# Token-MLP stretches of 25 and 23 filler matmuls, one paired row maximum, and output bursts in two halves

## The chip, the cores and the metric

The kernel runs on 1 core of a Trainium2 chip. The metric is the device time of one execution in microseconds (us). The kernel before was timed three times: 1595.57, 1595.95 and 1596.51, a median of 1595.95. One more execution was profiled and took 1596.58; its span, first instruction to last, is 1594.8.

## The reference, cut to what matters

```python
# S, D, H, F = 2048, 640, 32, 1728; Dh = 20
q = heads(x @ wq); k = x @ wk; v = x @ wv              # one k and one v for all 32 heads
scores = einsum("bhqd,bkd->bhqk", q, k) * Dh ** -0.5
a = rows(einsum("bhqk,bkd->bhqd", softmax(scores), v)) @ wo
h = layernorm(x)
u = gelu(einsum("bsd,sf->bdf", h, w1) + b1)             # MLP over the token axis
b = einsum("bdf,fs->bds", u, w2) + b2
out = g * a + (1 - g) * b                               # g = sigmoid(x . gate_w)
```

## The kernel before, in words

Attention and MLP are woven into one stream. Attention is cut into 512 units (32 blocks of 4 heads x 512 queries, 16 key blocks each), and the stream into 248 *stretches*. A stretch j holds matmuls of four kinds:

- **scores** (L689): keys against queries into one of seven PSUM banks, a tile of 128x512; ScalarE turns it into `p` by an exponential (L701). There are 8 in a stretch.
- **maxima** (L507): the same product with queries in front, so that VectorE can reduce 512 columns to one (`tensor_reduce`, L515). They serve a later block's softmax.
- **fillers**: MLP or output-projection matmuls of 320 columns (L1020 for MLP1, L845 for MLP2, L973 for the projection) into a bank `g` of their own.
- **the burst** (L725): `p` times V for two units, four heads side by side, into a bank that ScalarE then copies out (L749) and GpSimd adds up (L752).

Scores, maxima and fillers contract over 64 rows or fewer, so they use one half of the array's rows, and two run side by side. In stretch j the half j % 2 is the *own lane*: it takes the scores and most of the maxima. The other is the *filler lane*: all fillers and one to three maxima. A burst uses all rows, so both lanes end before it.

`ph` lists the fillers of each stretch. `batches` cuts each MLP1 tile (48 steps per lane) into two batches of 24, and each batch gives one stretch per lane: the 70 stretches j = 2 to 71 have 24 fillers each and want 10 maxima (`wants`). MLP2 stretches have 20 or 21 fillers, the projection's 15. `share` says how many maxima the own lane takes (8 of the 10 in MLP1), and `layout` writes each lane's order as a string: `s` score, `m` maximum, `f` filler, `SS` two scores in neighbouring banks with one exponential over 1024 columns. For MLP1 the string is fixed: `ssmSSmmssmssmmmm`.

`arrange` merges the two lanes into TensorE's one queue. It keeps a clock per lane, for VectorE and for ScalarE, and a time at which each bank is free (`free`), all from constants such as `EACH` (an engine's time for one instruction, and how long after its start the bank is free). It issues the lane whose next matmul could start first, in the bank that is free first. A reduction is put on VectorE's queue when its clock says so, or when its bank is taken again. After the last filler, `signal` puts a small memset (L711) on VectorE's queue, for which the next stretch's first filler waits. `burst` takes column ranges (`cuts`): MLP2 bursts are cut into two halves of 256 queries, each with a bank and a copy of its own; MLP1 bursts are whole.

Of the kernel before, what the change touches and what calls it, by code (L numbers as in the profile page):

```python
# [39 lines left out]
def mix_kernel(ctx: ExitStack, tc: tile.TileContext, A_x, A_wq, A_wk, A_wv, A_wo,  # L40
# [452 lines left out]
    def ms_next(b):  # L493
        k = given[b]
        if k >= 32 * NU or k // 32 not in qtiles:
            return None
        given[b] += 1
        n, r = divmod(k, 32)
        (kq, pr), qt = divmod(r // 4, 2), r % 4

        def step(i=None):
# [10 lines left out]
            out = mtiles[n][:, (2 * b + pr) * 4 + qt, kq:kq + 1]  # L512

            def reduce():
                red = nc.vector.tensor_reduce(out, ms, axis=AX.X, op=ALU.max)  # L515
                if region:
                    touch(red, reads=region)
                issued[b] += 1

            return reduce  # L520

        return step

    def ms_done():
# [504 lines left out]
    def batches(tiles, counts):  # L1029
        out = []  # L1030
        for n, (load, parts, *_) in enumerate(tiles):
            for d, (steps, done) in enumerate(parts):
                cnt = counts.pop(0)
                rows = [[f[h] for f in steps if len(f) > h] for h in range(2)]
                cut = [[len(r) * j // cnt for j in range(cnt + 1)] for r in rows]
                for j in range(cnt):
                    rest = []
                    if d == 0 and j == 0 and n + 1 < len(tiles):
                        rest.append(tiles[n + 1][0])
                    out.append(([r[c[j]:c[j + 1]] for r, c in zip(rows, cut)], rest, [done] if j == cnt - 1 else []))  # L1040
        return out

    n_st = (len(units) - TAIL) // 2
    todo = [divmod(i, FC) for i in range(PRO, 2 * FC)]
    seq = batches([b1_jobs(*t) for t in todo], [2] * len(todo))
    m = len(seq)
    seq += batches([b2_jobs(st) for st in range(NS)], [2] * 2 * NS)
    seq[-1][1].append(second)
# [28 lines left out]
        ph[j][1].append(lambda st=st: tail_load(st, 0, CUT))  # L1077
    ph[n_st - 8][1].append(move_wo)

    X_US, F_US, O_US = 0.2345, 0.1468, 0.869  # L1080
    W_US, FIRST_US, LAST_US, NEXT_US, SEEN_US = 0.11, 0.1, 0.333, 0.13, 0.43
    EACH = {"dve": (0.6, 0.84), "act": (0.48, 0.815)}
    PAIR_US = 0.85
    clock = {"dve": 0.0, "act": 0.0}
    lane, fresh, free = [0.0, 0.0], [True, True], [0.0] * 3 + [1.3] * 4
    state = {"at": 0.0, "f": 0.0, "last": 0.0}
# [13 lines left out]

    def begins(h, kind):
        at = max(lane[h] + W_US * fresh[h], state["at"])
        if kind == "S":
            return max(at, pair[1] if pair else free[next_pair()])
        return max(at, state["f"] if kind in "fe" else min(free))

    def issue(h, kind, f):
        at = state["at"] = begins(h, kind)
        fresh[h] = False
        lane[h] = at + (F_US if kind in "fae" else X_US)  # L1110
        state["last"] = at
        if kind in "fae":
            f()
        elif kind == "S":
            if not pair:
                i = next_pair()
                pair[:] = [i, free[i + 1]]
                free[i] = free[i + 1] = float("inf")
            else:
                i = pair[0] + 1  # L1120
                begin = spend("act", PAIR_US, at + SEEN_US) - PAIR_US
                free[i - 1] = free[i] = begin + PAIR_US + EACH["act"][1] - EACH["act"][0]
                pair.clear()
            while any(k == i for _, k, _ in reduces):
                reduces.pop(0)[2]()
            f(i)
# [12 lines left out]

    def layout(n_s, n_m, n_f, n_o):  # L1140
        if n_f > 22 and n_o > 1:
            places = [0, n_f]
        elif n_f > 22:
            places = [0]
        else:
            places = [0, n_f]
        places = (places + [n_f // 2, 3 * n_f // 4])[:n_o]
        lf = ""
        for i in range(n_f + 1):
            lf += "m" * places.count(i) + "f" * (i < n_f)  # L1150
        lf += "m" * (n_o - lf.count("m"))
        if n_f > 22 and (n_s, n_m, n_o) == (8, 8, 2):
            return "ssmSSmmssmssmmmm", lf
        lx = "sSS" if n_s + n_m > 12 else "s"
        s, m = n_s - len(lx), n_m
        a, b = s, m
        while s or m:
            if m and (not s or m * a >= s * b):
                lx, m = lx + "m", m - 1
            else:  # L1160
                lx, s = lx + "s", s - 1
        return lx, lf

    def arrange(h, ss, own, other, fs, end):
        ss, own, other, fs = list(ss), list(own), list(other), list(fs)
        n_s, n_m, n_f = len(ss), len(own), len(fs)
        lx, lf = layout(n_s, n_m, n_f, len(other))
        pairs.clear()
        at = lx.replace("m", "").find("S")
        if at >= 0:  # L1170
            pairs.update({at: 0, at + 1: 2})
        lx = [(k, (own if k == "m" else ss).pop(0)) for k in lx]
# [22 lines left out]
    def burst(us, cuts=(0, NB)):  # L1195
# [7 lines left out]
        for at, to in zip(cuts, cuts[1:]):  # L1203
# [9 lines left out]
            free[i] = spend("act", took, t + 0.25) + hold - each  # L1213
        lane[:] = [t + NEXT_US] * 2
        fresh[:] = [True, True]

# [25 lines left out]
    def share(j):  # L1242
        h, to = j % 2, owed + wants[j]
        own = round((min(to, 9) + F_US / X_US * len(ph[j][0]) - 8) / 2)
        if h:
            own = (given[0] - given[1] + to + 1) // 2
        own = min(to, max(0, own))
        return (to - own, own) if h else (own, to - own)

    for j in range(n_st):  # L1250
# [31 lines left out]
        w1_load(fetched[0] + 3)  # L1282
        for f in rest:
            f()
        spend("dve", 0.03)
        spend("act", 0.1)
# [192 lines left out]
```

## Time and profile before

| | us |
|---|---|
| median of three | 1595.95 |
| profiled execution | 1596.58 |
| its span | 1594.8 |
| 70 MLP1 stretches, 187.50 to 611.49 | 423.99 |
| MLP2 stretches, 617.06 to 1316.15 | 699.09 |
| VectorE busy in the MLP1 part | 422.70 |
| ScalarE busy in the MLP1 part | 333.18 |

TensorE counts as busy all the time, because the ends of matmuls are modelled and include their waits; so a stretch is read from starts: of its burst, of the first matmul behind it, of each lane's matmuls, and of the next burst. VectorE's and ScalarE's instructions overlap their successors a little, so what one costs in a full queue is the distance between starts, not its duration.

### The profile page before, as it was taken

Reading aid. Unit: us, or ns where it says so; the run is one execution under the profiler, and the core shown is the slowest. Engines: PE = TensorE matmul, PEld = TensorE weight load, DVE = VectorE, ACT = ScalarE, POOL = GpSimd, SP = SyncE. Lnnn points to the kernel's source line nnn. Section 1 sums busy time; section 2 is a strip of 40 time slices with the busy share of each in tenths; the row PEclk is TensorE's granted clock in tenths of the full one; section 3 lists DMA queues with packets and bytes.
Section 4 is the critical chain, followed back from the end, with each engine's and each line's share of the span. In section 5 each row is a group of like instructions: output and inputs, shape, how many; then the busy total and the mean of one; then the engine's idle time right before and its main releaser. Section 6 shows DMA issues by size and latency. Waiting matters only on the chain.

```text
span 1594.8 us, 43452 instructions
## 1 busy us (share of the span) xinstructions
PE 1587.7 (100%) x16907; PEld 1184.8 (74%) x16907; DVE 1381.2 (87%) x2626; ACT 1295.5 (81%) x2481; POOL 846.0 (53%) x930
## 2 busy tenths in 40 slices
PE   9999999999999999999999999999999999999998
PEld 7799867767676777777777777777777776666665
DVE  6689999999999999999999999999999996677743
ACT  4445678778787788888888888888888889999996
POOL 6558767777777777545544344444444433333340
PEclk9999999999999999999999999999999999999999
DMA  7665322232222221322112122122211113322341
GB/s 213 204 173 144 97 60 71 66 75 69 77 64 70 61 76 54 93 70 66 52 55 58 53 61 58 55 61 62 62 54 49 48 49 101 118 84 83 90 138 59
DMA packets 180452, 129.78 MB, mean 81 GB/s; under 512 B 41617, under 2 KB 150062, under 8 KB 180246
## 3 DMA queue, kind: packets, MB, share of 16 engines
q1 hardware_dynamic: 179958, 126.68, 28.4%
q8 instruction: 133, 2.18, 0.6%
q14 instruction: 73, 0.60, 0.1%
q10 hardware_dynamic: 288, 0.33, 0.1%
HBM read 93.57 MB, written 32.15 MB: 79 GB/s over the span
## 4 chain that ended last, share of the span: by engine, by line
PE 97%; DVE 1%; SPq 1%; DMA 1%; POOL 0%; ACT 0%; issue 0%; DVEq 0%
PE xs L725 30%; PE xs L689 18%; PE xs L507 18%; PE g L845 11%; PE g L1020 7%; PE pu L634 4%; PE pp L303 3%; PE g L973 3%; PE x L507 1%; PE xs L927 1%; DMA xa<-in_A_x_dram 0%; DVE st L236 0%; SPq L200 0%; DMA q_scr<-ql 0%; PE pt L295 0%; DVE ht L255 0%
## 5 line engine op out<-in xcount | busy, mean ns | idle before, releaser
L515 DVE TENSOR_REDUCE mp<-xs 128x1 f32<-128x512 f32 x1946 | 1199.8, 683 | 130.2 <-PE xs L689 66.6
L701 ACT ACTIVATE p<-xs 128x512 f32<-128x512 f32 (+1 forms) x1841 | 1016.1, 674 | 7.3 <-PE xs L689 3.4
L752 POOL TENSOR_TENSOR osum<-osum,part 128x512 f32<-128x512 f32 x216 | 279.7, 1295 | 594.2 <-ACT part L749 577.6
L725 PE MATMUL xs<-p,v_sb 128*32 128x256 f32 (+1 forms) x6144 | 493.6, 454 | 0.0
L689 PE MATMUL xs<-q,kst 62*128 62x512 f32 x1344 | 474.0, 416 | 0.0
L507 PE MATMUL xs<-kst,q 60*128 60x512 f32 x1242 | 432.9, 408 | 0.0
L725 PEld LDWEIGHTS xs<-p,v_sb 128*32 128x32 f32 x6144 | 173.6, 109 | 209.2 <-issue 80.9
L689 PEld LDWEIGHTS xs<-q,kst 62*128 62x128 f32 x1344 | 237.3, 185 | 57.1 <-DVE mp L515 30.2
L749 ACT ACTIVATE part<-xs 128x256 f32<-128x256 f32 (+1 forms) x328 | 149.1, 455 | 155.6 <-PE xs L725 154.2
L1020 PE MATMUL g<-slot,w 64*128 64x320 f32 x1728 | 266.1, 305 | 0.0
L1020 PEld LDWEIGHTS g<-slot,w 64*128 64x128 f32 x1728 | 258.9, 184 | 1.9
L507 PEld LDWEIGHTS xs<-kst,q 60*128 60x128 f32 x1242 | 214.0, 184 | 50.3 <-DVE mp L515 19.3
L127 POOL TENSOR_TENSOR w<-wr,w 128x512 fp32r<-128x512 f32 (+1 forms) x180 | 225.5, 1255 | 34.6 <-ACT w L124 17.5
L689 PE MATMUL xs<-slot,kst 62*128 62x512 f32 x569 | 207.5, 418 | 0.0
L507 PE MATMUL xs<-kst,slot 60*128 60x512 f32 x576 | 205.5, 408 | 0.0
L845 PE MATMUL g<-u,w 64*128 64x320 f32 x1296 | 200.4, 305 | 0.0
L845 PE MATMUL g<-slot,w 64*128 64x320 f32 x1296 | 200.3, 305 | 0.0
L845 PEld LDWEIGHTS g<-slot,w 64*128 64x128 f32 x1296 | 195.1, 184 | 1.7
L845 PEld LDWEIGHTS g<-u,w 64*128 64x128 f32 x1296 | 195.2, 184 | 1.6
L689 PEld LDWEIGHTS xs<-slot,kst 62*128 62x128 f32 x569 | 100.2, 185 | 19.9 <-ACT part L749 7.4
L507 PEld LDWEIGHTS xs<-kst,slot 60*128 60x128 f32 x576 | 99.7, 184 | 20.3 <-ACT part L749 9.9
L973 PE MATMUL g<-slot 64*128 64x320 f32 x720 | 113.5, 306 | 0.0
(190 smaller groups left out, 1446.4 us busy)
## 6 DMA issues: line engine op xcount, KB each, us to landing
wr<-in_B_w_dram SPq DMA_DIRECT2D x155, 256.0 KB
q<-q_scr SPq DMA_DIRECT2D x126, 80.0 KB
rb<-r_scr SPq DMA_DIRECT2D x120, 64.0 KB
slot<-o_scr SPq DMA_DIRECT2D x24, 320.0 KB
y_scr<-yo SPq DMA_DIRECT2D x16, 320.0 KB
q_scr<-qh SPq DMA_DIRECT2D x19, 256.0 KB
q_scr<-ql SPq DMA_DIRECT2D x19, 256.0 KB
o_scr<-rb SPq DMA_DIRECT2D x120, 40.0 KB
```

The costliest lines, as they stand in the source:

```text
L127: nc.gpsimd.tensor_sub(wl, wr, f32(wh))
L507: mm = nc.tensor.matmul(ms, qtiles[n][64 * b:64 * b + 60, pr, qt * P:(qt + 1) * P], kst[64 * b:64 * b + 60, kq * NB:(kq + 1) * NB], start= ...
L515: red = nc.vector.tensor_reduce(out, ms, axis=AX.X, op=ALU.max)
L634: nc.tensor.matmul(pu[r][:, :HD2], w[rows, c, :], h[rows, st, :], start=(st == 0 and k == 0), stop=(st == NS - 1 and k == 2))
L689: mm = nc.tensor.matmul(s, kst[64 * b:64 * b + 62, kb * P:(kb + 1) * P], q[64 * b:64 * b + 62, pr, :], start=True, stop=True)
L701: act = nc.scalar.activation(p_all[:, a * NB:(j + 1) * NB], s, AF.Exp, scale=SCALE)
L725: mm = nc.tensor.matmul(o[32 * hh:32 * hh + 32, at:to], v_sb[:, units[u][1], :], p_all[:, j * NB + at:j * NB + to], start=first, stop=last ...
L749: touch(nc.scalar.activation(t[:, at:to], o[:, at:to], AF.Copy), [("x", i)])
L752: nc.gpsimd.tensor_add(osum[n], osum[n], t)
L845: other_tile(half, nc.tensor.matmul(hold["p"][:, :HD2], w[r, fc % HS, :], u[d][r, fc, :], start=(hold["n"] == 1), stop=(hold["n"] == 6 * F ...
L973: other_tile(half, nc.tensor.matmul(hold["p"][:, :HD2], o[r, c, :], w[r, c, d * HD2:(d + 1) * HD2], start=(hold["n"] == 1), stop=(hold["n" ...
L1020: other_tile(half, nc.tensor.matmul(hold["p"][:, :HD2], w[r, st % HS, :], h[d][r, st, :], start=(hold["n"] == 1), stop=(hold["n"] == 6 * NS)))
```

## The change

It has these parts.

- `batches` cuts MLP1 tiles into 25 + 23 steps, so that stretches go 25, 25, 23, 23.
- `share` gives the own lane 9 of the 10 maxima beside 25 fillers, and 8 beside 23.
- `layout` has four fixed strings (`EARLY`), by number of fillers and lane. In each, `M` stands for two maxima in neighbouring banks with one `tensor_reduce` over 1024 columns and two outputs. No `SS` is left in MLP1. Where the pair would join two different query blocks' rows (`turns`), `M` changes places with an `m`.
- `burst` is cut into halves in MLP1 too.
- The planner's constants change: banks read by ScalarE are free 0.70 after its start (0.815 before), and others by some hundredths.

```diff
-                cut = [[len(r) * j // cnt for j in range(cnt + 1)] for r in rows]
+                cut = [[len(r) * j // cnt + more * (0 < j < cnt) for j in range(cnt + 1)] for r in rows]
...
+            both = part == 2
+            out = mtiles[n][:, col - both:col + 1, kq]
+            if both:
+                ms = span(i - 1, 2).rearrange("p (a k) -> p a k", a=2)
+                region.append(("x", i - 1))
...
-    X_US, F_US, O_US = 0.2345, 0.1468, 0.869
-    W_US, FIRST_US, LAST_US, NEXT_US, SEEN_US = 0.11, 0.1, 0.333, 0.13, 0.43
-    EACH = {"dve": (0.6, 0.84), "act": (0.48, 0.815)}
-    PAIR_US = 0.85
+    X_US, F_US, O_US = 0.2345, 0.1468, 0.862
+    W_US, FIRST_US, LAST_US, NEXT_US, SEEN_US = 0.11, 0.09, 0.333, 0.112, 0.43
+    EACH = {"dve": (0.598, 0.838), "act": (0.476, 0.70)}
+    PAIR_US = {"act": 0.903, "dve": 1.13}
...
+    EARLY = {(23, 0): "ssmsmssmmsmssMm", (23, 1): "ssmsmsmmsmsssMm",
+             (25, 0): "smsssmssmmmmssmM", (25, 1): "smsssmsmssmMmsmm"}
...
-        if n_f > 22 and (n_s, n_m, n_o) == (8, 8, 2):
-            return "ssmSSmmssmssmmmm", lf
+        if n_f > 22 and (n_s, n_m, n_o) == (8, 10 - n_o, n_o):
+            lx = list(EARLY[n_f, h])
+            at = lx.index("M")
+            if own[lx[:at].count("m")].turns:
+                to = at + 1 if "m" in lx[at:] else max(i for i in range(at) if lx[i] == "m")
+                lx[at], lx[to] = lx[to], lx[at]
+            return "".join(lx).replace("M", "MM"), lf
...
+        if len(ph[j][0]) > 22 and to == 10:
+            own = 8 + (len(ph[j][0]) > 24)
...
-            burst((2 * j - 2, 2 * j - 1), (0, NB // 2, NB) if 15 < len(ph[j][0]) <= 22 else (0, NB))
+            burst((2 * j - 2, 2 * j - 1), (0, NB // 2, NB) if len(ph[j][0]) > 15 else (0, NB))
```

TensorE's queue at the end of one MLP1 stretch, before. In all of these, L507 is a maximum, L689 (now L697) a score, L1020 (L1028) a filler, L725 (L733) the burst; `xs_2756` and `xs_2760` are banks 0 to 2 and 3 to 6.

```order
L507 MATMUL xs_2760<-kst,q 128x512
L1020 MATMUL g<-slot_80,w_90 128x320 x2
L507 MATMUL xs_2756<-kst,slot_79 128x512
L1020 MATMUL g<-slot_80,w_90 128x320
L507 MATMUL xs_2756<-kst,slot_79 128x512
L1020 MATMUL g<-slot_80,w_90 128x320 x2
L507 MATMUL xs_2760<-kst,slot_79 128x512
L507 MATMUL xs_2760<-kst,q 128x512
L725 MATMUL xs_2756<-p,v_sb 32x512 x8
```

The same place of the same stretch now, which is one of 25 fillers.

```order
L697 MATMUL xs_2756<-q,kst 128x512
L1028 MATMUL g<-slot_80,w_90 128x320
L507 MATMUL xs_2756<-kst,slot_79 128x512
L1028 MATMUL g<-slot_80,w_90 128x320 x2
L507 MATMUL xs_2760<-kst,slot_79 128x512
L1028 MATMUL g<-slot_80,w_90 128x320
L507 MATMUL xs_2760<-kst,slot_79 128x512
L1028 MATMUL g<-slot_80,w_92 128x320
L733 MATMUL xs_2760<-p,v_sb 32x256 x16
```

The filler lane now ends with a filler, and the last two maxima of the own lane (both in `xs_2760`) are the pair. The burst has 16 matmuls of 256 columns.

VectorE's queue over one MLP1 stretch, before, from memset to memset (L515 is the reduction).

```order
L711 MEMSET flag 1x1
L515 TENSOR_REDUCE mp<-xs_2760 128x1
L515 TENSOR_REDUCE mp<-xs_2756 128x1 x2
L515 TENSOR_REDUCE mp<-xs_2760 128x1 x2
L515 TENSOR_REDUCE mp<-xs_2756 128x1
L515 TENSOR_REDUCE mp<-xs_2760 128x1 x2
L515 TENSOR_REDUCE mp<-xs_2756 128x1
L515 TENSOR_REDUCE mp<-xs_2760 128x1
L711 MEMSET flag 1x1
```

And now (the reduction is L522, the memset L719).

```order
L719 MEMSET flag 1x1
L522 TENSOR_REDUCE mp<-xs_2760 128x2
L522 TENSOR_REDUCE mp<-xs_2760 128x1
L522 TENSOR_REDUCE mp<-xs_2756 128x1 x2
L522 TENSOR_REDUCE mp<-xs_2760 128x1
L522 TENSOR_REDUCE mp<-xs_2756 128x1
L522 TENSOR_REDUCE mp<-xs_2760 128x1
L522 TENSOR_REDUCE mp<-xs_2756 128x1
L522 TENSOR_REDUCE mp<-xs_2760 128x1
L719 MEMSET flag 1x1
```

Ten reductions became nine; the row `128x2` is the pair. In the MLP2 and projection stretches the four kinds of matmul follow each other as before, in partly other banks. In the last eight visits, which a random search over the planner's clock orders, the order differs.

## Rows read from the trace of the kernel before

**Rows 1.** The page: busy time by engine over the whole span.
```profile
PE 1587.7 (100%) x16907; PEld 1184.8 (74%) x16907; DVE 1381.2 (87%) x2626; ACT 1295.5 (81%) x2481; POOL 846.0 (53%) x930
```

**Rows 2.** Busy time by stretch of time: MLP1, then MLP2.
```profile
core 0: us, PE busy (x) PEld busy (x) DVE busy (x) ACT busy (x) POOL busy (x), PEclk, DMA share, GB/s
187.50:611.49 423.99, 423.99 (x4062) 300.09 (x4061) 422.70 (x799) 333.18 (x614) 306.70 (x362) 1.00 0.26 67
617.06:1316.15 699.09, 699.09 (x8671) 543.45 (x8669) 637.62 (x1193) 614.73 (x1176) 326.24 (x353) 1.00 0.21 59
```

**Rows 3.** Timeline of VectorE in MLP1: start, length, instruction, count.
```profile
364.31 6.08 DVE L515 TENSOR_REDUCE mp<-xs 128x1 f32<-128x512 f32 x10
369.71 0.06 DVE L711 MEMSET flag<- 1x1 f32 x1
```

**Rows 4.** Timeline of TensorE over one MLP1 stretch.
```profile
363.10 1.92 PE L725 MATMUL xs<-p,v_sb 128*32 128x512 f32 x16
364.95 0.50 PE L507 MATMUL xs<-kst,slot 60*128 60x512 f32 x1
364.96 0.73 PE L689 MATMUL xs<-q,kst 62*128 62x512 f32 x2
365.29 0.45 PE L1020 MATMUL g<-slot,w 64*128 64x320 f32 x2
...
367.17 0.39 PE L507 MATMUL xs<-kst,slot 60*128 60x512 f32 x1
...
367.43 0.49 PE L689 MATMUL xs<-q,kst 62*128 62x512 f32 x1
...
367.77 0.43 PE L689 MATMUL xs<-q,kst 62*128 62x512 f32 x1
...
368.54 0.45 PE L1020 MATMUL g<-slot,w 64*128 64x320 f32 x2
368.74 0.48 PE L507 MATMUL xs<-kst,slot 60*128 60x512 f32 x2
369.16 1.06 PE L725 MATMUL xs<-p,v_sb 128*32 128x512 f32 x8
```

**Rows 5.** The same in MLP2, with a burst in halves.
```profile
771.20 1.93 PE L725 MATMUL xs<-p,v_sb 128*32 128x256 f32 x32
773.06 0.50 PE L507 MATMUL xs<-kst,slot 60*128 60x512 f32 x1
...
776.67 1.07 PE L725 MATMUL xs<-p,v_sb 128*32 128x256 f32 x16
```

**Rows 6.** The same late in the kernel: a lane that ends with three fillers.
```profile
1536.75 0.60 PE L973 MATMUL g<-slot 64*128 64x320 f32 x3
1537.28 0.64 PE L725 MATMUL xs<-p,v_sb 128*32 128x512 f32 x4
```

**Rows 7.** Groups by shape: duration (ns) of reductions, exponentials and copies.
```profile
L515 DVE TENSOR_REDUCE mp<-xs 128x1 f32<-128x512 f32 x1946 | 1199.8, 683 | 130.2 <-PE xs L689 66.6 <-PE xs L507 62.9
L701 ACT ACTIVATE p<-xs 128x512 f32<-128x512 f32 x1641 | 856.4, 630 | 7.2 <-PE xs L689 3.4
L701 ACT ACTIVATE p<-xs 128x1024 f32<-128x1024 f32 x200 | 206.0, 1030 | 0.1
L749 ACT ACTIVATE part<-xs 128x256 f32<-128x256 f32 x224 | 86.2, 385 | 69.9 <-PE xs L725 69.7
L537 DVE TENSOR_REDUCE mm<-mp 128x16 f32<-128x64 f32 x32 | 6.7, 210 | 0.1
```

**Rows 8.** Timeline of ScalarE behind a burst: whole in MLP1, in halves in MLP2.
```profile
365.15 0.60 ACT L749 ACTIVATE part<-xs 128x512 f32<-128x512 f32 x1 [1.62 <-PE xs L725]
365.64 3.96 ACT L701 ACTIVATE p<-xs 128x512 f32<-128x512 f32 x7
...
778.67 0.39 ACT L749 ACTIVATE part<-xs 128x256 f32<-128x256 f32 x1 [0.42 <-PE xs L725]
779.07 1.52 ACT L701 ACTIVATE p<-xs 128x512 f32<-128x512 f32 x2
```

More of the change, by code (lines that the diff above doesn't have):

```diff
@@ L499, in ms_next, with step @@
         (kq, pr), qt = divmod(r // 4, 2), r % 4
-        def step(i=None):
+        def step(i=None, part=0):
             if n not in mtiles:
@@ L511, in step @@
                 touch(mm, writes=region)
-            out = mtiles[n][:, (2 * b + pr) * 4 + qt, kq:kq + 1]
+            col = (2 * b + pr) * 4 + qt
+            if part == 1:
+                return None
+            both = part == 2
[3 more added lines that the diff above has]
+                region.append(("x", i - 1))
             def reduce():
@@ L517, in reduce @@
                     touch(red, reads=region)
-                issued[b] += 1
+                issued[b] += 1 + both
             return reduce
+        step.turns = r % 8 == 7
         return step
@@ L1027, in b1_jobs, with batches @@
                         for st in range(NS) for k in range(3)], done)]
-    def batches(tiles, counts):
+    def batches(tiles, counts, more=0):
         out = []
@@ L1044, in mix_kernel @@
     todo = [divmod(i, FC) for i in range(PRO, 2 * FC)]
-    seq = batches([b1_jobs(*t) for t in todo], [2] * len(todo))
+    seq = batches([b1_jobs(*t) for t in todo], [2] * len(todo), 1)
     m = len(seq)
@@ L1102, in begins @@
         at = max(lane[h] + W_US * fresh[h], state["at"])
-        if kind == "S":
+        if kind in "SM":
             return max(at, pair[1] if pair else free[next_pair()])
@@ L1113, in issue @@
             f()
-        elif kind == "S":
+        elif kind in "SM":
+            e = "act" if kind == "S" else "dve"
             if not pair:
@@ L1120, in issue @@
                 i = pair[0] + 1
-                begin = spend("act", PAIR_US, at + SEEN_US) - PAIR_US
-                free[i - 1] = free[i] = begin + PAIR_US + EACH["act"][1] - EACH["act"][0]
-                pair.clear()
+                begin = spend(e, PAIR_US[e], at + SEEN_US) - PAIR_US[e]
+                free[i - 1] = free[i] = begin + PAIR_US[e] + EACH[e][1] - EACH[e][0]
+                pair.append(begin)
             while any(k == i for _, k, _ in reduces):
                 reduces.pop(0)[2]()
-            f(i)
+            if kind == "S":
+                f(i)
+            else:
+                g = f(i, len(pair) - 1)
+                if g:
+                    reduces.extend(((begin, i - 1, g), (begin, i, lambda: None)))
+            if len(pair) > 2:
+                pair.clear()
         else:
@@ L1138, in mix_kernel, with layout @@
     pairs = {}
-    def layout(n_s, n_m, n_f, n_o):
+    EARLY = {(23, 0): "ssmsmssmmsmssMm", (23, 1): "ssmsmsmmsmsssMm",
+             (25, 0): "smsssmssmmmmssmM", (25, 1): "smsssmsmssmMmsmm"}
+    def layout(h, n_s, own, n_f, n_o):
+        n_m = len(own)
         if n_f > 22 and n_o > 1:
@@ L1165, in arrange @@
         ss, own, other, fs = list(ss), list(own), list(other), list(fs)
-        n_s, n_m, n_f = len(ss), len(own), len(fs)
-        lx, lf = layout(n_s, n_m, n_f, len(other))
+        n_f = len(fs)
+        lx, lf = layout(h, len(ss), own, n_f, len(other))
         pairs.clear()
-        at = lx.replace("m", "").find("S")
+        at = lx.replace("m", "").replace("M", "").find("S")
         if at >= 0:
             pairs.update({at: 0, at + 1: 2})
-        lx = [(k, (own if k == "m" else ss).pop(0)) for k in lx]
+        lx = [(k, (own if k in "mM" else ss).pop(0)) for k in lx]
         lf = [(k, (other if k == "m" else fs).pop(0)) for k in lf]
@@ L1212, in burst @@
             took = each * (to - at) / NB + 0.05 * (to - at < NB)
-            free[i] = spend("act", took, t + 0.25) + hold - each
+            free[i] = spend("act", took, t + 0.31) + hold - each
         lane[:] = [t + NEXT_US] * 2
@@ L1284, in mix_kernel @@
             f()
-        spend("dve", 0.03)
-        spend("act", 0.1)
+        spend("dve", 0.06)
+        spend("act", 0.02)
         if j == 8 * 25 - 1:
```

## The prediction

> **What bounds the kernel now.** I read the page's busy times first, then the same times by stage, then one MLP1 stretch on VectorE and on TensorE, and then the rows that price what the trace of before does not hold. Over the whole span VectorE is busy 87% and ScalarE 81% [rows 1], which decides nothing. By stage it is plainer: in the MLP1 part VectorE is busy 422.70 of 423.99 us, ScalarE only 333.18 [rows 2]. This part is 70 stretches, 423.99 / 70 = 6.057 us each. In MLP2 VectorE is busy 637.62 of 699.09, so it has room there.
>
> The reader is to see in VectorE's timeline ten reductions that take 6.08 us without a break, and the memset inside them [rows 3]. One lasts 683 ns [rows 7], so the distance from start to start is (6.08 - 0.68) / 9 = 0.600. Ten of them are 6.00; the memset and the small reductions, transposes and reciprocals of the softmax fill the rest of 6.057.
>
> TensorE is just as tight, which is why neither bound alone may be moved. In its timeline [rows 4] the burst starts at 363.10, the first maximum at 364.95 (1.85 later), the first filler at 365.29 (0.34 on). The last two fillers start at 368.54 and 368.69, so 24 fillers are (368.69 - 365.29) / 23 = 0.148 apart, without a stop. Then one maximum, and the next burst 0.33 after its start: the filler lane sets these 6.06 us. The own lane's matmuls are (367.17 - 365.30) / 8 = 0.234 apart, and it has slack: 1.85 + 0.34 + 14 x 0.234 + 0.33 = 5.80 for its sixteen. In that slack lies a wait: the score at 367.43 lasts 0.49 instead of 0.39 and starts 0.03 late, and the next one comes 0.34 after it, 0.11 late.
>
> **The pair.** It replaces two reductions. The trace has no reduction of 1024 columns, so I bound its saving. From 64 to 512 columns a reduction grows from 210 to 683 ns [rows 7], 1.056 ns a column. One of 1024 should last 683 + 512 x 1.056 = 1224, and, starting its successor 83 ns before its end as the others do, occupy 1.14. Two singles occupy 1.20: saved 0.06 per stretch. From below: nothing, if a second bank costs what a second instruction costs. From above: the whole fixed part, 210 - 64 x 1.056 = 142 ns. I take 0.06, the row of the same operation. VectorE's share of a stretch becomes 6.057 - 0.06 = 6.00.
>
> [...] Rows 3 and 7 show that part of the fixed time is already hidden, as starts are 83 ns closer than durations. [...]
>
> **25 and 23 fillers.** I walk both lanes with the distances above, and the burst in halves: in MLP2 the first matmul starts 773.06 - 771.20 = 1.86 after such a burst [rows 5], 0.01 more than in MLP1. That is 0.7 us in 70 stretches, and it is in the walk.
>
> - 25 fillers: the own lane has seventeen matmuls, 1.86 + 0.34 + 15 x 0.234 = 5.71 for the start of the last, and 0.33 to the burst: 6.04. The filler lane ends with a filler at 1.86 + 0.34 + 24 x 0.148 = 5.75; where a lane ends with fillers the burst starts 1537.28 - 1537.04 = 0.24 after the last one's start [rows 6], so 5.99. The own lane sets 6.04.
> - 23 fillers: the filler lane is 6.06 less one filler of 0.148, plus 0.01: 5.92. The own lane's sixteen end at 5.81.
>
> The mean is 5.98 for TensorE, against 6.06. So both bounds fall by about the same. VectorE wants 6.00 in every stretch. If it carries its queue from the 23s, where TensorE runs ahead, into the 25s, the mean is 6.00. If it carries nothing, a 25 takes 6.04 and a 23 takes 6.00, mean 6.02. I take 6.01.
>
> **ScalarE.** With a burst in halves the second copy starts at 778.67 and the first exponential at 779.07, 0.54 after the first score's start (778.53, which is 1.86 after the burst's 776.67 [rows 5]); with a whole one the exponential starts at 365.64, 0.69 after it [rows 8]. So its chain starts 0.15 earlier. It loses the pair `SS`: six singles and one pair take 3.96 [rows 8], which is six distances, one of them 0.40 longer as a pair lasts 400 ns more [rows 7], and a last duration of 0.63, so a distance is (3.96 - 0.40 - 0.63) / 6 = 0.49 and eight singles cost 0.49 - 0.40 = 0.09 more. A second copy of 385 ns instead of one of 600 lies in the 1.62 that ScalarE waits for the burst [rows 8]. ScalarE ends no later, and I cost this at nothing. If that cover were gone (exponentials late by 0.1 at the end of a 23, so that the burst waits for its bank), half of the stretches would be 0.1 longer, 3.5 us.
>
> **Queues and what stays.** The memset that each stretch's first filler needs now follows a last filler that starts 5.75 after the burst's start instead of 5.59. In rows 3 it runs at 369.71, 1.0 behind the start of the last filler of rows 4, as reductions stand before it; with 0.16 less nobody waits yet. Without that queue VectorE would stand until the filler ends, some 0.1. POOL's adds and SP's transfers keep their order in MLP1, and POOL is idle a quarter of this part [rows 2]. In MLP2 and the projection the order of kinds is the same, and banks differ. MLP2's stretch of 5.47 (771.20 to 776.67) is the filler lane's, so another bank gains nothing; I allow 0.5 us either way for it and for the reordered tail.
>
> **The sum.** (6.057 - 6.01) x 70 = 3.3 us. From the profiled execution (span 1594.8, 1.78 around it, 1596.58) that is 1593.3. The median of before is 0.63 below that execution, so I predict 1592.7. Less than 0.2% (3.2 us) can't be told from no change here.
>
> **Rivals.**
>
> 1. *The own lane stops in the 25s* (slower). Its slack of 0.26 is gone there: 6.04 is the longest lane. The wait in rows 4 costs 0.03 + 0.11 = 0.14 whatever it is for, and today it is free. The pair wants two neighbouring banks at the same time and holds both until it ends, 1.2 us, and the planner now counts a bank free 0.115 earlier after an exponential: both make waits likelier. With two such stops in each 25 (6.32) and one in each 23 (5.95), the mean is 6.135, 70 x 0.078 = 5.5 us slower, 1601.4. For it speaks that the stretch of rows 4 has such a stop; against it, that today's stop has a cause that goes: VectorE's queue is full, and a bank comes late. It decides from a mean above 6.10, that is from stops of over 0.2 us in a 25.
>    [...]
> 2. *One stop in each 25* (no change). 6.04 + 0.14 = 6.18, and 5.95 in the 23s, mean 6.065: 1596.5. Half of that, 6.03, gives 1594.1. The same comes out where the pair saves nothing and VectorE still needs 6.057, so that the change does not do what it says: 1596.0. For it speaks that the margins are hundredths; against it, that the pair reads the same columns with one start less.
> 3. *TensorE alone sets the time* (more gain). The pair saves 0.1 or more, VectorE falls behind no more, and the mean is 5.98: 5.4 us, 1590.5. For it speaks that MLP2 runs at its filler lane's pace to 0.01; against it, rows 3 and 7.
>
> **How the numbers follow.** Forecast (6.00 to 6.03) 0.40; rival 1 0.12; rival 2 0.28; rival 3 0.20. The forecast's own range is 1592.0 to 1594.1, across the bound of 0.2%, which lies at a mean of 6.011; three quarters of it fall on the faster side. So faster 0.30 + 0.20 = 0.50, same 0.10 + 0.28 = 0.38, slower 0.12. The range reaches from rival 3 with 0.3 more for the tail, 1590.2, through rival 2, to 1597.5, and leaves out most of rival 1.
>
> **What would show it.** In the profile after, starts of bursts in MLP1 should alternate two by two: 6.04 twice and 5.92 to 6.00 twice. A `tensor_reduce` from 128x1024 should appear 70 times at about 1224 ns, and its successor start some 1.14 after it; over 1.19 and the pair saves nothing. VectorE should still be without breaks, or nearly. The first exponential should start 0.54 behind the first score. Own lanes in the 25s should have no matmul that starts more than 0.26 after the one before, except behind the burst. MLP2 stretches should stay at 5.47. The prediction is wrong if the 25s are above 6.15, if the burst waits for banks in the 23s, or if the gain comes from outside the 70 stretches.

## The result

The changed kernel takes 1600.12 us (median of 10 runs, 1599.71 to 1600.43) against 1595.69 of the kernel before beside it (1595.48 to 1596.51): a ratio of 1.0026, 95% interval 1.0018 to 1.0034. It is slower by 4.4 us, where 1592.7, 3.3 us faster, was forecast and 1597.5 was the end of the range. The profiled execution took 1600.13, its span is 1598.4.

The busy times of the page, and those of the 70 MLP1 stretches (first burst to 71st), answer to [rows 1, 2].

```profile
PE 1591.6 (100%) x18043; PEld 1217.9 (76%) x18043; DVE 1380.7 (86%) x2556; ACT 1319.7 (83%) x2622; POOL 846.7 (53%) x930
```

```profile
187.74:614.90 427.16, 427.16 (x5180) 332.50 (x5179) 422.02 (x730) 354.97 (x753) 306.76 (x362) 1.00 0.26 67
```

MLP1 takes 427.16 instead of 423.99, so 3.17 of the 3.6 us between the spans are there: 6.102 a stretch, not 6.057. (The medians are 4.4 apart and not 3.6, because the profiled execution of before was 0.9 above the median of the ten timed here.) VectorE, which had 1.3 us to spare there, now has 5.1. It seems no longer to be the bound, and something else is longer; f4 below tests this. ScalarE's work there has grown by 22 us. The other parts moved by 0.3 us or less each (MLP2 699.38 against 699.09, the start of MLP1 by 0.24).

The mean of stretches 11 to 70, by place in the cycle of four: 25 fillers 6.156 and 6.193, 23 fillers 6.047 and 6.022. Forecast were 6.04 twice and 5.92 to 6.00 twice.

The groups of VectorE's reductions by shape, for [rows 7]: the long maximum lasts 1218 ns.

```profile
L522 DVE TENSOR_REDUCE mp<-xs 128x1 f32<-128x512 f32 x1806 | 1123.4, 683 | 134.1 <-PE xs L697 68.5 <-PE xs L507 63.2
L522 DVE TENSOR_REDUCE mp<-xs 128x2 f32<-128x1024 f32 x70 | 85.2, 1218 | 0.0
```

**A stretch of 25.** TensorE's timeline, for [rows 4]: the own lane's matmuls late in the stretch, and the bursts at both ends (start, length).

```profile
352.46 1.93 PE L733 MATMUL xs<-p,v_sb 128*32 128x256 f32 x32
354.32 0.50 PE L697 MATMUL xs<-q,kst 62*128 62x512 f32 x1
...
356.75 0.40 PE L507 MATMUL xs<-kst,q 60*128 60x512 f32 x1
...
357.01 0.50 PE L507 MATMUL xs<-kst,slot 60*128 60x512 f32 x1
357.01 0.56 PE L1028 MATMUL g<-slot,w 64*128 64x320 f32 x2
357.35 0.40 PE L507 MATMUL xs<-kst,slot 60*128 60x512 f32 x1
357.41 0.45 PE L1028 MATMUL g<-slot,w 64*128 64x320 f32 x2
...
358.33 0.39 PE L507 MATMUL xs<-kst,slot 60*128 60x512 f32 x1
358.66 0.62 PE L733 MATMUL xs<-p,v_sb 128*32 128x256 f32 x5
```

ScalarE's timeline beside it, for [rows 8]: the second copy of the burst, and the eight exponentials.

```profile
354.46 0.39 ACT L757 ACTIVATE part<-xs 128x256 f32<-128x256 f32 x1 [0.48 <-PE xs L733]
354.89 4.03 ACT L709 ACTIVATE p<-xs 128x512 f32<-128x512 f32 x8
```

The lane runs at 0.234 and then stops: 357.01 is 0.26 behind the one before, and 357.35 another 0.34. The bank of the matmul at 357.01 had held a score. The exponentials are (4.03 - 0.63) / 7 = 0.486 apart, so the fourth ends at 354.89 + 3 x 0.486 + 0.63 = 356.98, just when the lane wants its bank (356.75 + 0.234); the semaphore that this matmul waits for in the trace is that exponential's. This is the stop of rival 1 and rival 2, once in a 25; the other 25 has it one exponential later. The filler lane is late beside it: the two fillers of 357.01 take 0.56 together, and two without a stop take 0.45.

**A stretch of 23**, the next one: TensorE, then ScalarE.

```profile
358.66 1.93 PE L733 MATMUL xs<-p,v_sb 128*32 128x256 f32 x32
360.52 0.49 PE L697 MATMUL xs<-q,kst 62*128 62x512 f32 x1
...
364.27 0.44 PE L507 MATMUL xs<-kst,slot 60*128 60x512 f32 x2
364.70 0.42 PE L733 MATMUL xs<-p,v_sb 128*32 128x256 f32 x4
```

```profile
360.66 0.39 ACT L757 ACTIVATE part<-xs 128x256 f32<-128x256 f32 x1 [0.42 <-PE xs L733]
361.11 4.03 ACT L709 ACTIVATE p<-xs 128x512 f32<-128x512 f32 x8
```

The last two matmuls start at 364.27 and just behind. The burst should follow 0.33 later, at 364.61, and starts at 364.70. The bank it opens with was a score's: the stretch's seventh exponential ends at 361.11 + 6 x 0.486 + 0.63 = 364.66. So a 23 is as long as ScalarE's chain: 1.86 from the burst to the first score, 0.59 to the first exponential, 3.55 to the end of the seventh, 0.04 to the burst, 6.04. Fillers don't appear in this sum. The trace has the same in all thirty 23s from the eleventh stretch on: the burst waits for the seventh exponential and starts 0.05 after it ends. In the thirty 25s more than 0.2 lie between the two. The experiments test this reading.

### The profile page after: what moved, and what is told of

Its sections match the earlier page's. It is cut to its first block, busy times and chain, and to the rows that moved or that the text cites. A ratio compares the mean times of both kernels' runs of the same rounds, so it can differ in the third digit from the quotient of the medians.

```text
span 1598.4 us, 45968 instructions
## 1 busy us (share of the span) xinstructions
PE 1591.6 (100%) x18043; PEld 1217.9 (76%) x18043; DVE 1380.7 (86%) x2556; ACT 1319.7 (83%) x2622; POOL 846.7 (53%) x930
## 4 chain that ended last, share of the span: by engine, by line
PE 97%; SPq 1%; DMA 1%; DVE 0%; ACT 0%; issue 0%; DVEq 0%; ACTq 0%
PE xs L733 30%; PE xs L697 18%; PE xs L507 18%; PE g L853 11%; PE g L1028 7%; PE pu L642 4%; PE pp L303 3%; PE g L981 3%; PE xs L935 1%; PE x L507 0%; PE g L507 0%; DMA xa<-in_A_x_dram 0%; PE pt L295 0%; ACT p L709 0%; DVE st L236 0%; DMA q_scr<-ql 0%
## 5 line engine op out<-in xcount | busy, mean ns | idle before, releaser
L522 DVE TENSOR_REDUCE mp<-xs 128x1 f32<-128x512 f32 (+1 forms) x1876 | 1199.0, 703 | 134.1 <-PE xs L697 68.5
L733 PE MATMUL xs<-p,v_sb 128*32 128x256 f32 (+1 forms) x7280 | 494.3, 409 | 0.0
L697 PE MATMUL xs<-q,kst 62*128 62x512 f32 x1344 | 475.6, 412 | 0.4 <-ACT p L709 0.4
L507 PE MATMUL xs<-kst,q 60*128 60x512 f32 x1242 | 441.1, 413 | 0.0
L733 PEld LDWEIGHTS xs<-p,v_sb 128*32 128x32 f32 x7280 | 210.5, 109 | 206.1 <-ACT p L709 62.6
L697 PEld LDWEIGHTS xs<-q,kst 62*128 62x128 f32 x1344 | 241.2, 185 | 45.6 <-ACT part L757 16.9
L757 ACT ACTIVATE part<-xs 128x256 f32<-128x256 f32 (+1 forms) x390 | 159.3, 409 | 134.0 <-PE xs L733 132.7
L1028 PE MATMUL g<-slot,w 64*128 64x320 f32 x1728 | 268.2, 306 | 0.0
L1028 PEld LDWEIGHTS g<-slot,w 64*128 64x128 f32 x1728 | 259.3, 184 | 1.7
L507 PEld LDWEIGHTS xs<-kst,q 60*128 60x128 f32 x1242 | 209.3, 184 | 43.2 <-ACT part L757 25.9
L507 PE MATMUL xs<-kst,slot 60*128 60x512 f32 x576 | 208.0, 411 | 0.0
L697 PE MATMUL xs<-slot,kst 62*128 62x512 f32 x567 | 206.7, 416 | 0.0
L697 PEld LDWEIGHTS xs<-slot,kst 62*128 62x128 f32 x567 | 100.0, 185 | 18.6 <-ACT part L757 8.2
L507 PEld LDWEIGHTS xs<-kst,slot 60*128 60x128 f32 x576 | 98.4, 184 | 18.4 <-ACT part L757 12.3
```

Source lines behind the costliest of these rows:

```text
L697: mm = nc.tensor.matmul(s, kst[64 * b:64 * b + 62, kb * P:(kb + 1) * P], q[64 * b:64 * b + 62, pr, :], start=True, stop=True)
L733: mm = nc.tensor.matmul(o[32 * hh:32 * hh + 32, at:to], v_sb[:, units[u][1], :], p_all[:, j * NB + at:j * NB + to], start=first, stop=last ...
L757: touch(nc.scalar.activation(t[:, at:to], o[:, at:to], AF.Copy), [("x", i)])
L1028: other_tile(half, nc.tensor.matmul(hold["p"][:, :HD2], w[r, st % HS, :], h[d][r, st, :], start=(hold["n"] == 1), stop=(hold["n"] == 6 * NS)))
```

## The experiments

Times are medians beside the kernel before on the same chip, ratios with their 95% interval; the mean MLP1 stretch is from each profile.

| kernel | us | ratio | mean stretch |
|---|---|---|---|
| changed, the planner's old clock (e4) | 1604.12 | 1.0052 (1.0037 to 1.0067) | 6.167 |
| changed, whole bursts (e1) | 1626.74 | 1.0194 (1.0178 to 1.0209) | 6.474 |
| changed, 24 and 24 (e2) | 1602.82 | 1.0044 (1.0028 to 1.0061) | 6.150 |
| changed, no long maximum (e3) | 1599.85 | 1.0025 (1.0015 to 1.0035) | 6.093 |
| changed, bursts cut at 3/4 (e5) | 1600.71 | 1.0030 (1.0018 to 1.0042) | 6.102 |
| changed, more on ScalarE (e6) | 1599.50 | 1.0024 (1.0015 to 1.0034) | 6.089 |
| changed, more on VectorE (e7) | 1616.41 | 1.0129 (1.0114 to 1.0145) | 6.337 |
| before, more on ScalarE (e11) | 1600.52 | 1.0030 (1.0018 to 1.0041) | 6.122 |
| changed, one exponential halved (f1) | 1594.16 | 0.9990 (0.9980 to 0.9999) | 6.013 |
| f1, no long maximum (f2) | 1596.16 | 1.0002 (0.9992 to 1.0011) | 6.043 |
| before, one exponential halved (f3) | 1595.77 | 0.9999 (0.9990 to 1.0009) | 6.052 |
| changed, one maximum halved (f4) | 1600.09 | 1.0027 (1.0016 to 1.0037) | 6.104 |
| before, single exponentials (g1) | 1599.27 | 1.0020 (1.0011 to 1.0030) | 6.099 |
| g1 and halves (g2) | 1595.58 | 0.9997 (0.9987 to 1.0006) | 6.053 |
| g2 and 25 + 23 (h2) | 1599.17 | 1.0021 (1.0011 to 1.0031) | 6.101 |
| changed, another order (g4) | 1600.81 | 1.0030 (1.0019 to 1.0041) | 6.111 |

### One part undone

```diff
e4   EARLY, split, pair, halves stay; all of X_US ... PAIR_US, spend() and t + 0.31 as before
e1   -(0, NB // 2, NB) if len(ph[j][0]) > 15
     +(0, NB // 2, NB) if 15 < len(ph[j][0]) <= 22
e2   -seq = batches([b1_jobs(*t) for t in todo], [2] * len(todo), 1)
     +seq = batches([b1_jobs(*t) for t in todo], [2] * len(todo))     # the strings of the 23s
e3   -return "".join(lx).replace("M", "MM"), lf
     +return "".join(lx).replace("M", "mm"), lf
```

> The changed kernel with all the constants of the planner's clock put back to the old ones (a bank that ScalarE reads is held 0.815 again and not 0.70, VectorE's 0.84, the eviction is counted from 0.25 behind the burst and not 0.31, ScalarE is charged 0.1 between stretches and not 0.02); split, 1024-wide maximum and halves stay. Before: mean MLP1 stretch 6.058, 1595.7; changed 6.102, 1600.1. Theory 1, the clock: in the 23-stretches the burst waits 0.09 to 0.13 for a bank that the 7th exponential frees, and in the 25-stretches the pair's first bank comes late by a stop of 0.12 to 0.15, because the new clock counts ScalarE's banks about 0.1 too early; then these waits go, stretches of 6.03 and 5.92, mean 5.98 to 6.00, total 1592 to 1593.5. Theory 2, the lanes: a lane of 17 without slack stops whatever the clock says, and ScalarE is as late as before; 6.09 to 6.12, 1599 to 1601. Theory 3, another place: the old clock costs the other stages what the new one gave them, MLP1 gains no more than 0.03 a stretch, 1598 to 1600.

> The changed kernel with the bursts of MLP1 whole again (one bank of 512, one eviction); all else stays. Theory 1, the clock: halves help, since the last eviction behind a burst is 0.39 long and not the whole one's 0.57 or so, so ScalarE's chain of eight exponentials starts 0.15 later here and every bank it frees is later by as much: the 23s wait 0.25 for the bank of their burst, mean 6.15 to 6.22, total 1604 to 1608. Theory 4, the halves: the second bank and second eviction (0.2 more of ScalarE's time in a stretch) are what made ScalarE late; then the mean falls to 6.02 to 6.05 and the total to 1595 to 1597.

> The changed kernel with 24 fillers in every MLP1 stretch (16 score and maximum matmuls in the own lane, 24 fillers and 2 maxima in the other), with the pair, the halves and the new clock. Theory 2, the lanes: no lane is without slack in its own half any more, the filler lane of 24 and 2 ends 0.147 later than that of a 23-stretch, 5.75 behind the burst's start, plus 0.32: 6.07 with no wait anywhere, total 1597.5 to 1598.5. Theory 1, the clock: the same 0.147 gives the 7th exponential the time that it lacks in the 23s, so the burst's wait goes here too, 6.06 to 6.08; what tells the two apart is whether any wait for a ScalarE bank is left inside the lanes (then 6.10 and more, 1600 or above).

> The changed kernel with the pair's two matmuls followed by two maxima over 512 columns again instead of one over 1024. Theory 3, the pair: the pair needs two neighbouring banks at one place of the lane and holds both for 1.22, and the stops of the 25s stand there; without it those stops go (25s at 6.04), VectorE binds again by 10 maxima of 0.598 or so plus the flag: mean 6.05 to 6.07, total 1596 to 1597.5. Theory 1, the clock: the 23s wait for ScalarE's bank as before and VectorE's 0.07 comes back on top of the chain: 6.10 to 6.14, total 1600 to 1603.

None gave the time back. My first theory, the planner's clock, fell with e4: three of the four kinds of stretch kept their length to 0.01 (6.046, 6.021, 6.16), and the fourth went from 6.19 to 6.49 on average. The banks now come in another order, and the pair's second bank is not free when its first is. Two rows of e4's TensorE show it: the second half of the pair waits for an exponential and starts 1.00 after the first.

```profile
357.97 0.39 PE L507 MATMUL xs<-kst,slot 60*128 60x512 f32 x1
358.97 0.50 PE L507 MATMUL xs<-kst,slot 60*128 60x512 f32 x1
```

The same befell e2, whose pair is split by up to 0.56, here by the wait for a reduction:

```profile
364.36 0.46 PE L507 MATMUL xs<-kst,slot 60*128 60x512 f32 x1
364.92 0.50 PE L507 MATMUL xs<-kst,slot 60*128 60x512 f32 x1
```

So e2, 4 us above what either theory had for it without a wait, does not say what the split costs; that was run again as h2. e1, 19 us above the worst that was expected, gives stretches from 6.13 to 6.96; it mixes a later ScalarE and a new order, and which of them weighs more was not tested. e3 is clean: without the pair the 25s keep 6.16 and 6.19, so the pair is not what stops the lane, and the mean does not rise, so the time that VectorE saves by the pair decides nothing. One of the 23s even falls, from 6.047 to 6.002; e6 below shows the same.

### More work on one engine

```diff
e5   +(0, 3 * NB // 4, NB) if len(ph[j][0]) > 22          # cuts of the burst
e6, e11, behind burst():
     +nc.scalar.activation(spare[:, 0, :], spare[:, 1, :], AF.Copy)
e7, ahead of burst():
     +nc.vector.tensor_copy(spare[:, 0, :], spare[:, 1, :])
```

> The changed kernel with the bursts of MLP1 cut at three quarters of the queries instead of half (first part 384 columns, second 128), the order of the work otherwise the same. The second eviction, behind which ScalarE's eight exponentials stand, is then of 128 columns and not 256: shorter by 0.05 to 0.1, so the chain of exponentials starts that much earlier. Theory S, ScalarE's chain (burst 1.86 to the first score, 0.59 to the first exponential, seven exponentials of 0.50 to the bank that the next burst needs: 6.03 for the 23-stretches; in the 25s the 5th exponential's bank comes 0.05 after its matmul wants it and costs the lane 0.12 to 0.15): the 23s fall from 6.045 and 6.022 to 5.94 to 5.99, the 25s from 6.156 and 6.193 to 6.06 to 6.13, MLP1 mean 6.02 to 6.05, total 1594 to 1596.5. Theory V, VectorE: it gives no bank earlier, all four stay within 0.02, total 1599.5 to 1600.5. Theory H, the halves themselves (two banks for a burst): no change either, or worse.

> The changed kernel with one small copy more on ScalarE (128 x 16) between the second eviction and the first exponential of each MLP1 stretch, 0.1 to 0.2 of ScalarE's time. Theory S, ScalarE's chain: each stretch grows by all of it, 23s and 25s, 7 to 14 us in MLP1, total 1607 to 1614. Theory V, VectorE's maxima or theory L, TensorE's lane of 17 matmuls, set the length: ScalarE has 72 us of idle time in MLP1's 427, the copy goes into it, total within 2 us of 1600.

> The changed kernel with one small copy more on VectorE (128 x 16, 0.06 to 0.1 of its time) in each MLP1 stretch. Theory S: VectorE's gaps, some 0.07 to 0.2 in a stretch, take it up in part, MLP1 grows by 0 to 3 us, total 1600 to 1603. Theory V: VectorE's 9 maxima and the long one are still what the stretch waits for, and all of the copy comes on top: 4 to 7 us, total 1604 to 1607.

> The kernel before with the same small copy more on ScalarE behind the burst's eviction in each MLP1 stretch. It tells whether ScalarE's work was covered there, as the prediction had it. Theory S with a lost cover: before, VectorE set the 6.06 and ScalarE had slack of its own (its pair of exponentials, its stretches of 24 fillers), so the 0.1 to 0.2 costs 0 to 0.06 a stretch, total 1595.7 to 1600. If ScalarE's chain was as tight before as after, the whole of it comes on top: 1603 to 1610.

By my expectations e5 and e6 spoke against ScalarE: its theory had 1594 to 1596.5 for e5 and 1607 to 1614 for e6. The traces say why they could not speak. ScalarE in e6 (start, length), whose stretch has its first score at 360.08:

```profile
360.22 0.38 ACT L759 ACTIVATE part<-xs 128x256 f32<-128x256 f32 x1 [0.48 <-PE xs L735]
360.50 0.21 ACT L1320 ACTIVATE spare<-spare 128x16 f32<-128x16 f32 x1
360.62 4.03 ACT L711 ACTIVATE p<-xs 128x512 f32<-128x512 f32 x8
```

The first exponential starts 0.54 after its score, no later than without the copy (0.53 to 0.59 in the four kinds of stretch): with halves its last wait is for its score, not for the eviction, and both edits fell into that wait. One 23 even got shorter, 5.993 against 6.047. There the changed kernel's first exponential waits for two semaphores, TensorE's and that of ScalarE's own eviction, and starts 0.594 behind its score; in e6, and in e3 and h2 too, it waits for TensorE's alone and starts 0.535 behind it. That is the whole difference, and the chain from there on is the same. In the kernel before, with a whole eviction, the first exponential does wait for the eviction: there the copy shows between the eviction and the exponentials (e11). They start 0.60 behind the eviction's start, not 0.49 as in [rows 8], 0.11 later, and the stretch is 6.122 - 6.057 = 0.065 longer.

```profile
366.23 0.60 ACT L751 ACTIVATE part<-xs 128x512 f32<-128x512 f32 x1 [1.61 <-PE xs L727]
366.72 0.21 ACT L1294 ACTIVATE spare<-spare 128x16 f32<-128x16 f32 x1
366.83 3.95 ACT L703 ACTIVATE p<-xs 128x512 f32<-128x512 f32 x7
```

So ScalarE had hardly 0.05 to spare already before: 0.11 - 0.065. e7 is spoilt: its copy lasts 0.16 in most stretches, and the 23s, where it nearly always does, keep their length (6.07, 6.02), but over half a microsecond in 19 of 72. Each of these 19 ends 0.03 to 0.05 after a GpSimd instruction; in the row below it is one from 354.11 to 355.39.

```profile
354.39 1.04 DVE L1315 COPY spare<-spare 128x16 f32<-128x16 f32 x1
```

```profile
354.11 1.28 POOL L127 TENSOR_TENSOR w<-wr,w 128x512 fp32r<-128x512 f32 x1
```

The copy ends at 355.43, 0.04 after that instruction; whether that instruction held it was not tested.

### Less work on one engine

The clean form takes time away from an engine without another order. f1 to f3 leave out half of one softmax tile in a stretch (f3 in 64 of the 70), so they are there for their times and compute something else; f4 leaves half a tile out of one maximum.

```diff
f1, f2, f3, in qk(), for one of the eight scores of an MLP1 stretch:
     -act = nc.scalar.activation(p_all[:, a * NB:(j + 1) * NB], s, AF.Exp, scale=SCALE)
     +act = nc.scalar.activation(p_all[:, a * NB:a * NB + NB // 2], s[:, :NB // 2], AF.Exp, scale=SCALE)
f2   +return "".join(lx).replace("M", "mm"), lf
f4, in step(), for the third own maximum:
     -red = nc.vector.tensor_reduce(out, ms, axis=AX.X, op=ALU.max)
     +red = nc.vector.tensor_reduce(out, ms[:, :NB // 2], axis=AX.X, op=ALU.max)
```

> The changed kernel with the third of the eight exponentials of each MLP1 stretch done over 256 of its 512 columns (the other half of that tile is left out), all else in the same order: 0.25 less of ScalarE's time ahead of the 5th and the 7th exponential. Theory S, ScalarE's chain from the first score: it runs without a gap, 0.54 from the first score and 0.49 for each exponential; the 5th frees the bank on which the lane of the 25s stops, the 7th the one that the 23s' burst takes, each 0.05 to 0.15 too late. Both stops go: 25s at 6.03 to 6.05, 23s at 5.90 to 6.00, MLP1 mean 5.98 to 6.01, total 1592 to 1594: what was forecast for the change. Theory V, VectorE: it hands its banks back no earlier, 6.08 to 6.10, total 1598.5 to 1600. Theory L, the lane of 17 stops by itself: only the 23s gain, mean 6.04, total 1596.

> The same short third exponential, and two maxima over 512 columns in the place of the one over 1024. Without the short one the pair was worth nothing (1599.85 against 1600.12). Theory S: with ScalarE out of the way VectorE sets the length, ten maxima of 0.598 and the flag's 0.06, 6.04 to 6.07, so the pair is now worth the 0.06 that the prediction gave it: total 1596.5 to 1598. Theory L or any other in which VectorE has room to spare: as the short exponential alone, 1592 to 1594.

> The kernel before with one exponential of each MLP1 stretch (the first behind the pair) done over half of its columns, the other half left out. The small copy on ScalarE cost the kernel before 0.065 a stretch, so its ScalarE had hardly any room; this tells whether it was the bound. VectorE (or TensorE's lane of 24 fillers and 2 maxima) the bound before, ScalarE just behind: nothing gained, 6.04 to 6.06, total 1594.5 to 1595.8. ScalarE the bound before as well: 6.00 or less, 1592 or less.

> The changed kernel with the third maximum of the own half in each MLP1 stretch taken over 256 of its 512 columns (the other half left out), all else in the same order: 0.26 less of VectorE's time ahead of the stops. Theory S: the banks on which lane and burst stop are ScalarE's, so nothing moves, mean 6.08 to 6.11, total 1598.5 to 1600.5. Theory V: VectorE's banks decide, stops go and the mean falls to 5.98 to 6.03, 1591.5 to 1595.

All four came out on the side of ScalarE's chain, f3 and f4 within its ranges, f1 and f2 0.2 and 0.3 us beside them (1594.16 for 1592 to 1594, 1596.16 for 1596.5 to 1598). MLP1 by engine in f1, and then in f4, with the columns of [rows 2]:

```profile
189.04:609.94 420.90, 420.90 (x5180) 334.55 (x5179) 418.79 (x728) 345.76 (x753) 306.25 (x362) 1.00 0.27 68
```

```profile
187.25:614.54 427.29, 427.29 (x5179) 332.08 (x5178) 409.32 (x730) 354.94 (x753) 306.63 (x362) 1.00 0.26 67
```

Taking 9 us from ScalarE shortens MLP1 by 6.3. Taking 13 us from VectorE shortens it by nothing. In f1 VectorE is again busy almost without a break, 418.79 of 420.90, as the prediction had it. There the 25s are 6.064 and 6.033, the 23s 5.995 and 5.968. The stop in the 25 is gone: TensorE's lane at the place shown above runs on at 0.23, and the stretch takes 6.01.

```profile
351.30 1.93 PE L735 MATMUL xs<-p,v_sb 128*32 128x256 f32 x32
...
355.60 0.39 PE L507 MATMUL xs<-kst,q 60*128 60x512 f32 x1
355.83 0.39 PE L507 MATMUL xs<-kst,slot 60*128 60x512 f32 x1
356.06 0.39 PE L507 MATMUL xs<-kst,slot 60*128 60x512 f32 x1
...
357.31 0.42 PE L735 MATMUL xs<-p,v_sb 128*32 128x256 f32 x4
```

f1 against f2 prices the long maximum once ScalarE is out of the way: 0.030 a stretch, 2.0 us, half of the 0.06 forecast. And f3 says that the kernel before gains nothing (6.052): ScalarE was close behind there, but not the bound.

### The change put together, one part at a time

```diff
g1, on the kernel before:
     -return "ssmSSmmssmssmmmm", lf
     +return "ssmssmmssmssmmmm", lf
g2   +burst(..., (0, NB // 2, NB) if len(ph[j][0]) > 15 else (0, NB))
h2   +cut = [[... + more * (0 < j < cnt) ...                       # 25 + 23, and
     +own = 8 + (len(ph[j][0]) > 24)                               # one more "m" in the 25s
g4, on the changed kernel:
     +EARLY = {(23, 0): "ssmsmsmssmssmmmm", (23, 1): "ssmsmsmsmmsmsmms",
     +         (25, 0): "sssmsmmsmsmsmmmms", (25, 1): "sssmsmmmssMsmsmm"}
     +"dve": (0.598, 0.81), "act": (0.485, 0.66), SEEN_US 0.49     # and spend() 0.03, 0.06
```

> The kernel before with its pair of exponentials in the MLP1 stretches (one over 1024 columns) done as two over 512; nothing else is changed. The change took this pair away along with all it added. It saves ScalarE 0.08 to 0.09 a stretch (3.96 for six and the pair against 4.03 for eight, and one start less). Theory P, the lost pair is what brought ScalarE's chain to the bound: the kernel before, whose ScalarE had no more than a hundredth or two to spare (a copy of 0.07 on it cost 0.065), then loses 0.05 to 0.09 a stretch as the changed kernel does; mean 6.11 to 6.15, total 1599 to 1602. Theory Q, the chain binds only at the faster pace that the split asks: within 0.02 of 6.057, total 1595 to 1597.

> The same, and the bursts of MLP1 in halves: the old stretches of 24 with eight single exponentials, halves, the old clock, no pair of either kind. Theory S: the halves take the eviction out of the way of the first exponential (0.54 from the first score, where the whole eviction makes it 0.65), which gives back the 0.06 to 0.1 that the lost pair cost; VectorE's ten maxima then set 6.05 to 6.08, total 1595.5 to 1597.5. If the halves give nothing back: as without them.

> The stretches of 24 with single exponentials, halves and the old clock (1595.58, 6.053 a stretch), and the split into 25 and 23 fillers alone, with 9 own maxima in the 25s; no pair of either kind, old clock. Theory S: ScalarE's chain does not shorten with the fillers, so the 23s stay at its length, 6.00 to 6.04, while the lane of 17 in the 25s stops once at the 5th exponential's bank, 6.16 to 6.20; mean 6.09 to 6.11, total 1598 to 1600: the split alone then costs what the changed kernel lost. Theory L', TensorE sets the length as the prediction had it: 6.04 and 5.92 with VectorE's ten maxima behind them, 6.05 at most, total 1595.5 or less.

> The changed kernel with another order in the own lanes of its stretches (scores and maxima set so that the lane asks later for the banks that ScalarE frees; the long maximum in one of the four stretches alone, single ones elsewhere) and with the planner's constants at which this order was chosen. Theory S, the 25s' stop in the lane is a matter of which bank comes when: that stop shrinks, 25s at 6.10 to 6.15, 23s as before at 6.00 to 6.04, mean 6.05 to 6.08, total 1596.5 to 1598.5. Theory L, a lane of 17 stops in whatever order: 25s stay at 6.16 to 6.19, total 1599.5 to 1601.

g1, g2 and h2 are steps of one ladder: 6.057 before, 6.099 without the exponentials' pair, 6.053 with halves, 6.101 with the split; the pair of maxima, the new orders and the new clock together end at 6.102. So single exponentials cost 0.042, halves give 0.045 back, and the split costs 0.047, 3.3 us, on its own. In g1 all sixty bursts from the eleventh stretch on start 0.05 after the seventh exponential; in g2, with the halves, none is so close. g1's timelines (TensorE, ScalarE) have the chain in full:

```profile
363.99 1.92 PE L725 MATMUL xs<-p,v_sb 128*32 128x512 f32 x16
365.84 0.49 PE L507 MATMUL xs<-kst,slot 60*128 60x512 f32 x1
365.85 0.50 PE L689 MATMUL xs<-q,kst 62*128 62x512 f32 x1
...
369.70 0.43 PE L507 MATMUL xs<-kst,slot 60*128 60x512 f32 x1
370.12 1.92 PE L725 MATMUL xs<-p,v_sb 128*32 128x512 f32 x16
```

```profile
366.53 4.02 ACT L701 ACTIVATE p<-xs 128x512 f32<-128x512 f32 x8
```

The first exponential starts 0.68 behind its score, the seventh ends at 366.53 + 6 x 0.485 + 0.63 = 370.07, and the burst starts at 370.12, 0.09 later than the last matmul asks. h2 has neither pair, and the planner's old clock, and its 25s stop too. TensorE's own lane in one of them, and ScalarE:

```profile
357.24 0.39 PE L507 MATMUL xs<-kst,slot 60*128 60x512 f32 x1
357.50 0.50 PE L507 MATMUL xs<-kst,slot 60*128 60x512 f32 x1
357.83 0.39 PE L507 MATMUL xs<-kst,slot 60*128 60x512 f32 x1
```

```profile
354.40 4.03 ACT L709 ACTIVATE p<-xs 128x512 f32<-128x512 f32 x8
```

The sixth exponential ends at 354.40 + 5 x 0.486 + 0.63 = 357.46, 0.04 before the matmul of 357.50. In h2's other 25 the stop is VectorE's: the matmul of 350.84 waits for a reduction that ends at 350.79, and the next in its lane starts 0.34 later. h2's 25s take 6.199 and 6.191, its 23s 5.996 and 6.030. In g4, with another order, the stop stands at another matmul, and the 25s keep 6.162 and 6.196: the expectation that an order would shrink it was wrong. In every order that was tried, a lane of 17 at 0.234 came to a bank that was not yet free: ScalarE's in the changed kernel, VectorE's in one of the two 25s of h2 (the reduction that ends at 350.79). f1 shows that it is the banks, not the lane's length.

No version was found that beats both kernels: g2, the best that computes all, is not to be told from the kernel before.

## Why the prediction was wrong

- **The pair.** Forecast 1224 ns, with its successor 1.14 after its start; it lasts 1218, and its successor starts 1.13 or 1.14 after it in 53 of 70. VectorE did fall below 6.06, and f4 shows that it is no longer the bound. This step held in its mechanism; where VectorE is the bound (f1 against f2) the saving is 0.03 and not 0.06. In the change it is worth nothing, because VectorE was not alone.
- **ScalarE, the step that failed.** "ScalarE ends no later, and I cost this at nothing." It compared the chain with where it had ended, not with when its banks would be wanted. The size was right, as what the lost pair `SS` cost (0.042) the halves gave back (0.045). But a 23 wants the burst's bank 0.14 earlier (5.92 instead of 6.06), and e11 shows that there was no such room. The rows on record had it: the last but one of the seven exponential instructions of [rows 8] ends at 365.64 + 3.96 - 0.49 = 369.11, and the burst of [rows 4], which was put down to the filler lane alone, starts at 369.16. The trace of before has the burst that close behind in 26 of 60 stretches. The chain is a floor that fewer fillers don't lower. The same sentence named the price if the cover were gone, half of the stretches 0.1 longer, 3.5 us: that is the 6.02 to 6.05 measured for 5.92.
- **The 25s.** "The own lane sets 6.04" walked it without a stop. There is one, as in rival 2, and it is what rival 2 said: 6.18 forecast, 6.156 and 6.193 measured. It is the larger part of the miss: 0.13 in 35 stretches is 4.7 us, against 1.2 us for 23s of 6.035 where VectorE's 6.00 was expected. The stop of [rows 4] waits for VectorE, and rival 1's "against" was right that this cause goes; the stops that came wait for exponentials. Rival 1 was right that the time would be slower, but the 25s don't stop twice, and the planner's clock and the pair, which it named as causes, are cleared by e4, e3 and h2, whose 25s stop all the same.
- **The sum.** Rival 2's 1596.5 and the price of the lost cover, 3.5, make 1600.0; measured 1600.12. Each was weighed as if it came alone. Both are one thing, ScalarE's chain seen at two places, so they come together, and the range should have held their sum. That the sum is so near is luck in part: it stands for a mean of 6.115, and the trace has 6.102. With the chain shortened (f1) the mean is 6.013, where 6.01 was forecast.
- **Halves.** The first exponential was forecast 0.54 behind the first score and is 0.57 to 0.59 in the two stretches above (0.53 to 0.59 in the four kinds). g1 to g2 shows what they are worth, 0.045.
- **The rest.** MLP2 moved by 0.3 us as allowed. Two of the prediction's own signs of being wrong came: 25s above 6.15, and a burst that waits for its bank in the 23s. The chances had a slip: of the range 1592.0 to 1594.1 only what lies below 1592.75 is the faster side, about a third and not three quarters.

Left open: why the matmul behind a late one starts 0.34 after it and not 0.234 (seen at the stops shown in full above; nothing was run on it), and why the first exponential of one 23 waits for its own engine's eviction in the changed kernel and not in e3, e6 and h2.

## What to carry to other kernels

Before calling a chain covered, hold its end against the new deadline, not against the old end, and look in the trace of before at what each burst waits for last: an engine that is busy 83% of a stage can still set the length of its stretches if its chain starts with the stretch and others wait for its buffers. Moving work from one stretch to the next helps only if every engine's work moves along; here the fillers were split 25 and 23, the exponentials stayed 8 and 8, and the long stretch paid while the short one could gain only 0.02. To find the bound, take a little work away from one engine and leave the order alone: adding work may fall into a wait, and undoing a part may set off another order.

## What the hardware showed that was not expected

- ScalarE's exponentials over 512 columns last 627 ns on average and start 0.48 to 0.49 apart, so each overlaps the next by some 0.14 us. VectorE's reductions overlap by 0.083 [rows 3, 7].
- In the rows above a stop costs more than its wait: the waiting matmul starts 0.02 to 0.03 late, at 0.26 behind the one before, and the next in its lane loses another 0.10, at 0.34.
- A copy of 16 columns on VectorE took 1.04 us beside a GpSimd instruction, where most take 0.16, and its stretch is 0.88 longer (7.03 against 6.156).
